# Another route for the decayed k of two attention units, and five smaller moves, in a gated linear attention and SwiGLU kernel on one core

## The chip, the cores and the metric

The kernel runs on one core of one Trainium2 chip. The metric is the device time of one execution in microseconds (us). The core has TensorE (PE in the profile, its weight loads PEld), VectorE (DVE), ScalarE (ACT), GpSimd (POOL) and SyncE (SP). SP, ACT and POOL also issue DMAs; each issues its own in program order.

## The reference, cut to what matters

All inputs to the attention are float32, the three weights float64. The attention is a recurrence with a decay for each channel; its output, with the heads side by side, is the input of a SwiGLU block.

```python
batch, n_heads, seq, head_dim = 4, 8, 768, 48
f = 1 / (1 + exp(-f_logit))
for t in range(S):
    state = f[:, :, t, :, None] * state + k[:, :, t] (x) v[:, :, t]
    y[:, :, t] = q[:, :, t] @ state
x = y.transpose(0, 2, 1, 3).reshape(3072, 384)
g = x @ w_gate                      # 384 x 1536
out = (g * sigmoid(g) * (x @ w_val)) @ w_out      # 1536 x 384
```

## The kernel before, in words

**Units.** The sequence is cut into six chunks c of 128 positions. A unit u = 4c + b is one chunk of one batch entry, all eight heads. The function `attention(u)` is a generator with some fifteen steps, so that the steps of a unit can be laid between the matrix products of the SwiGLU block for the chunk before. The steps are: sigmoid of f; f into the layout with channels on partitions; k likewise; a product scan from the back (`tail`, L630); kT, the k decayed to the end of its chunk (L576); the further route of kT for `turned` units (L646 to L650); a scan from the front (`gate`, L658); q into the layout; qT (L576 again); the scores kT against qT (L676); the causal mask on the scores (L691); the decayed state (L581); the output y (L712 and L716, or L737); the state's increment dS (L757), which needs kT with positions on partitions again, the tile `kt`; the new state (L766).

**Two routes to kt.** For a unit that isn't `turned`, four TensorE transposes (L680) put kT into a PSUM bank and ScalarE copies it to `kt` (L689). For a `turned` unit, VectorE transposes kT in blocks of 32 x 32 into the room that k was loaded to (`beside`, L646), four DMAs write it to DRAM (L649), and one DMA reads it back into `kt` in the right order (L687), issued in the step of the mask. In the kernel before, units 6 and 7 (GpSimd's queue) and 12 to 19 (SyncE's queue) are turned, units 0 to 5 and 8 to 11 are not, and the last chunk, 20 to 23, needs no `kt`. There is one `kt` buffer, so that its next writer waits for dS of the unit before. As `beside` lies in k's room, the k of the next unit is loaded (`load_after(u, "k")`) after the DMAs of L649 have read it, or right after the transpose of k (L622) where a unit isn't turned.

**The first stage (about 0 to 29 us)** runs the four units of chunk 0 with loads of f, k, q and v for each unit from SyncE's queue, and starts to fetch the weights. The weights come as float64; `weight_piece` turns each piece into float32 by ScalarE (L489, L491) and VectorE (the `join`: L500, L502, L504, then the sum L506 into w_both or w_out). Its order is written out by hand: `in_order` chains all instructions of TensorE, VectorE, ScalarE and SyncE as they are traced. GpSimd isn't in that chain; its instructions, such as the loads of v for units 6 and 7 (L455), are placed by the framework's own planned times.

**The second stage (about 29 to 140 us)** is the SwiGLU block of chunk 0 by plain products (`mlp_plain`: L812 for gate and val, L822 and L826 behind them, L835 for w_out), the rest of the weight pieces, sums of weights (L915, L918), and the units 4 to 7. Only a few of its instructions are chained by `keep_order` and `behind`; the rest is ordered by the framework's planned times.

**The third stage (from about 140 us)** does the SwiGLU block of chunks 1 to 5 by a fast matrix product: fifteen products of quarters and their sums for gate and val (`triple`, L1014, L1019, L915, L918, with L1030 and L966 behind them), in four rounds, then the product with w_out in seven parts (`down_seven`: one, six, two, three, four, five, seven, each in two halves; L1113 and L1176). Beside chunk c's block run the attention units of chunk c + 1. The order is by hand again, from a table of due times: each product counts 0.86, each half of a part of `down_seven` 1.95, and everything in `waiting` is traced when the sum of these has reached its time.

```python
    between = [n * TRIPLE - 0.05 for n in range(NJ)]                          # NJ = 4, TRIPLE = 12.9
    down = [NJ * TRIPLE + n * DOWN / 2 - 0.05 for n in range(14)]             # DOWN = 3.9
    return [[f, *steps, s + 0.02, s + masks[kind], s + 2.2, o, o + 0.01, o + 2.1] ...
    waiting += [(at, f) for at, f in zip(DOWN_SUMS_AT, down_weight_sums())]
```

`s` is a unit's time for the scores in `SCORES`, and also the time at which the output of the unit before is due (`o` of unit u is `s` of unit u + 1). `kind` says which PSUM banks the scores use: "A" are the two banks that the products and part three of `down_seven` also use. `SCORES` of the third chunk (c = 2) are 12, between[2], down[2] and down[6] for b = 0 to 3. `CHAINS` gives the times of the steps ahead of the scores. `down_weight_sums` makes four sums of halves of w_out (L918, tiles `ws` and w_out in place, 128 x 1152 each), which `down_seven` needs; they are due at `DOWN_SUMS_AT`. `in_order` chains TensorE, VectorE, ScalarE, GpSimd and SyncE in this stage as traced.

Of the kernel before, what the change touches and what calls it, by code (L numbers as in the profile page):

```python
# [9 lines left out]
FP32 = mybir.dt.float32  # L10
# [280 lines left out]
def short_path(ctx, tc, ident, least, judge, q, k, v, f_logit, moe_w_gate, moe_w_val, moe_w_out, out):  # L291
# [9 lines left out]
    nc = tc.nc  # L301
    B, H, S, D = q.shape
    C = 128
    NCH = S // C
    HP = H // 2
    W = 64
    DM = H * D
# [8 lines left out]
    SQUARES = 2  # L316
# [3 lines left out]
    att = ctx.enter_context(tc.tile_pool(name="att", bufs=1))  # L320
# [43 lines left out]
    def pairs(t, off=0):  # L364
        return t[:, off:off + HP * N1].rearrange("p (a t) -> p a t", t=N1)
# [35 lines left out]
    def by_squares(u):  # L401
        return u >= SQUARES * B - 2
# [6 lines left out]
    def v_of(u):  # L409
        return vs[u % (NV if units[u][1] < SQUARES else NV // 2)]  # L410
# [16 lines left out]

    traced = nc.cur_bb.bb.instructions
    by_pool = []

    def load(u, what="fkqv"):
        b, c = units[u]
        rows = slice(c * C, (c + 1) * C)
        inputs = dict(f=f_logit, k=k, q=q, v=v)
        for nm in "fqkv" if c >= SQUARES else "fvkq" if by_squares(u) else "fkqv":
            src = inputs[nm]
            if nm not in what:
                continue
            if nm == "v":
                dst = v_of(u)  # L440
            elif not by_squares(u):
                dst = raw[nm][u % NRAW]
            else:
                since = len(traced)
                for n in range(4):
                    at = Q * (1 - n % 2)
                    (nc.sync if c >= SQUARES else nc.gpsimd).dma_start(
                        out=rooms[nm][Q * n:Q * (n + 1), at:at + HP * RUN].rearrange("t (a e) -> t a e", a=HP),
                        in_=src[b, n // 2::2, rows, :].rearrange("a (t i) d -> t a (i d)", i=NI))
                if c < SQUARES:  # L450
                    by_pool.extend(ins for ins in traced[since:] if ins.engine == mybir.EngineType.Pool)
                    keep_order(by_pool[-5:])
                continue
            queue = nc.gpsimd if c < SQUARES and by_squares(u) else nc.sync
            queue.dma_start(out=dst[:, :, 0:D], in_=src[b, :, rows, :].rearrange("h t d -> t h d"))  # L455

    def weight_piece(dst, src, parts):

        b, a, n = dst.shape[1:]
        if src.dtype == FP32:
            by_row = src.rearrange("p a (b n) -> p a b n", n=n)
            return (lambda: [nc.sync.dma_start(out=dst[:, :, i], in_=by_row[:, i]) for i in range(a)]), [], []
        shape = [128, b // parts, a, n]
        kept = {}

        def fetch():  # L470
            kept["w"] = wst.tile([128, a, 2 * b * n], I32, tag="w64", name="w64", bufs=4)
            nc.sync.dma_start(out=kept["w"], in_=src)

        def part(m):
            return slice(m * b // parts, (m + 1) * b // parts)

        def halves(m):
            words = kept["w"].rearrange("p a (b n two) -> p a b n two", two=2, n=n)[:, :, part(m)].rearrange("p a b n two -> p b a n two")
            return words[:, :, :, :, 0], words[:, :, :, :, 1]

        def high_ends(m):
            quarters = kept["w"].bitcast(U16).rearrange("p a (b n four) -> p a b n four", four=4, n=n)[:, :, part(m)]
            return quarters.rearrange("p a b n four -> p b a n four")[:, :, :, :, 3]

        def sizes(m):
            lo, hi = halves(m)
            up = wst.tile(shape, I32, tag="up", name="up", bufs=NPART)
            ends = up.bitcast(U16).rearrange("p b a (n two) -> p b a n two", two=2)
            nc.scalar.activation(ends[:, :, :, :, 0], lo.bitcast(U32), AF.Copy, scale=2.0 ** -29)  # L489
            top = wst.tile(shape, I32, tag="top", name="top", bufs=NPART)  # L490
            nc.scalar.activation(top.bitcast(FP32), hi.bitcast(FP32), AF.Abs)  # L491
            kept["up", m], kept["top", m] = up, top

        def join(m, what=("clamp", "add")):
            lo, hi = halves(m)
            up, top = kept["up", m], kept["top", m]
            if "add" in what and "clamp" not in what:
                nc.vector.tensor_tensor(dst[:, part(m)].bitcast(I32), top, up, ALU.add)
                return
            nc.vector.tensor_scalar(top.bitcast(FP32), top.bitcast(FP32), as_float(0x38000000), as_float(0x47F00000),  # L500
                                    op0=ALU.max, op1=ALU.min)
            nc.vector.tensor_scalar(top, top, 3, 0x3FFFFFFF, op0=ALU.logical_shift_left, op1=ALU.bitwise_and)  # L502
            ends = up.bitcast(U16).rearrange("p b a (n two) -> p b a n two", two=2)
            nc.vector.tensor_single_scalar(ends[:, :, :, :, 1], high_ends(m), 0xC000, op=ALU.bitwise_and)  # L504
            if "add" in what:
                nc.vector.tensor_tensor(dst[:, part(m)].bitcast(I32), top, up, ALU.add)  # L506

        return fetch, [lambda m=m: sizes(m) for m in range(parts)], [lambda *what, m=m: join(m, *what) for m in range(parts)]

    def as_float(bits):  # L510
# [49 lines left out]
    def attention(u):  # L560
        b, c = units[u]
# [6 lines left out]
        in_squares = by_squares(u)  # L568

        def multiply(out, x, by):  # L570

            if in_squares:
                for_each = "p a (t j i) -> p a t j i"
                out, by = (t.rearrange(for_each, j=2, i=NI // 2) for t in (out, by))
                x = x.rearrange("p (j a t i) -> p a t j i", j=2, a=HP, i=NI // 2)
            nc.vector.tensor_tensor(out, x, by, ALU.mult)  # L576
# [35 lines left out]
            load_after(u, "f")  # L612
        yield

        turned = SQUARES < c < NCH - 1 or c < SQUARES and in_squares
        turn_queue = nc.sync if c >= SQUARES else nc.gpsimd
        kT = att.tile([128, HP, C], FP32, tag="kT", name="kT")
        qT = att.tile([128, HP, C], FP32, tag="qT", name="qT", bufs=2)
# [8 lines left out]
        n = HP * N1  # L627
# [14 lines left out]
        if turned:  # L642
# [4 lines left out]
            turn = turn_pool.tile([Q, NI, HP, NI, Q], FP32, tag="turn", name="turn")  # L647
            for r in range(NI):
                turn_queue.dma_start(out=turn[:, :, :, r, :].rearrange("t i a e -> t (i a) e"),  # L649
                                  in_=beside[Q * r:Q * (r + 1)].rearrange("t i (a e) -> t (i a) e", e=Q))  # L650
# [12 lines left out]
            load_after(u, "qv" if c < SQUARES else "q")  # L663
        yield
        multiply(qT, qp, pairs(gate)[:, :, 1:N1])
        nc.gpsimd.memset(pairs(gate)[:, :, 0:1], 0.0)  # L666
        if c < SQUARES:
            decay()
# [2 lines left out]
        A = att.tile([128, 2, HP, C], FP32, tag="A", name="A")  # L671
        sc = [score_bank(u) for _ in range(2)]
        for a in range(HP):
            for par in range(2):
                r = rows_of(par)
                nc.tensor.matmul(sc[par][:, a * C:(a + 1) * C], lhsT=kT[r, a, :], rhs=qT[r, a, :], start=True, stop=True)  # L676
        if c < NCH - 1 and not turned:
            p = bank("kt")
            for a in range(HP):
                nc.tensor.transpose(p[:, a * C:(a + 1) * C], kT[:, a, :], ident)  # L680
        yield
        if not in_squares:
            nc.scalar.copy(least[:, u, :], whole.rearrange("p a t -> p (a t)"))
        if c < NCH - 1:
            kt = att.tile([128, HP * C], FP32, tag="kt", name="kt")
            if turned:
                turn_queue.dma_start(out=kt, in_=turn.rearrange("t i a r e -> i t (a r e)"))  # L687
            else:
                nc.scalar.copy(kt, p)  # L689
# [10 lines left out]
        if c and b < B - 1:  # L700
# [8 lines left out]
            for a in range(HP):  # L709
                for par in range(2):  # L710
                    r = rows_of(par)
# [9 lines left out]
            for h in range(H):  # L721
                a, par = h // 2, h % 2
                f = h * D
                while f < (h + 1) * D:
                    n = min((h + 1) * D, (f // 128 + 1) * 128) - f
                    r = W * (a % 2) + f - h * D
                    (nc.gpsimd if c >= SQUARES else nc.sync).dma_start(out=xT[c][f % 128:f % 128 + n, f // 128, b * C:(b + 1) * C],  # L727
                                                                       in_=yT[r:r + n, par, a // 2 * C:(a // 2 + 1) * C])
# [60 lines left out]
    def keep_order(mine):  # L789
        for a, b in zip(mine, mine[1:]):  # L790
            tc.add_manual_dep(b, a.name, mybir.DependencyInfo(mybir.DependencyClass.NoSync,
                                                              mybir.DependencyReason.DATA), reason="order")
# [86 lines left out]
    def chain(k, q, qmul, turn=None, head=None):  # L879
# [3 lines left out]
    between = [n * TRIPLE - 0.05 for n in range(NJ)]  # L883
    down = [NJ * TRIPLE + n * DOWN / 2 - 0.05 for n in range(14)]
    SCORES = {c: scores for c, scores in zip(range(2, NCH), (
        ((12, "b"), (between[2], "o"), (down[2], "A"), (down[6], "A")),
        ((PRODUCT - 0.05, "b"), (between[1], "o"), (between[3], "o"), (down[3], "A")),
        *[((down[10] - whole, "A"), (between[1], "o"), (between[3], "o"), (down[3], "A"))] * (NCH - 4)))}
    CHAINS = {c: chains for c, chains in zip(range(2, NCH), (
# [18 lines left out]
        return {"o": banks_o, "A": banks_a}[kind].tile([128, 512], FP32, tag=kind, name="sc")  # L908

    FINISH = (3, 5, 6, 7, 9, 10)  # L910
    DOWN_SUMS_AT = (13.1, 26.5, 38, 48)
    sums = {}

    def plus(dst, a, b):
# [408 lines left out]

    waiting += [(at, f) for at, f in zip(DOWN_SUMS_AT, down_weight_sums())]
    blocks = {}
# [100 lines left out]
```

## Time and profile before

| what | us |
|---|---|
| median of three runs (600.44, 600.48, 600.49) | 600.48 |
| the profiled execution's own time | 600.68 |
| its span, first to last instruction | 599.0 |
| PE busy | 588.3 |
| DVE busy | 481.7 |
| ACT busy | 293.6 |
| POOL busy | 94.3 |

The span is what the profile's rows divide; the profiled execution took 1.7 us more than its span. Matmuls are pipelined and the profile models their ends, so that a row's busy time or mean duration is longer than the distance from one matmul to the next. For TensorE the start times of successive rows in the timeline are the measure. A timeline row is: start in us, duration in us, engine, line, operation, written tile <- read tiles, shape, count of merged instructions, and in brackets the idle time ahead of it with what ended it.

### The profile page before, as it was taken

Reading aid. Unit: us, or ns where it says so; the run is one execution under the profiler, and the core shown is the slowest. Engines: PE = TensorE matmul, PEld = TensorE weight load, DVE = VectorE, ACT = ScalarE, POOL = GpSimd, SP = SyncE. Lnnn points to the kernel's source line nnn. Section 1 sums busy time; section 2 is a strip of 40 time slices with the busy share of each in tenths; the row PEclk is TensorE's granted clock in tenths of the full one; section 3 lists DMA queues with packets and bytes.
Section 4 is the critical chain, followed back from the end, with each engine's and each line's share of the span. In section 5 each row is a group of like instructions: output and inputs, shape, how many; then the busy total and the mean of one; then the engine's idle time right before and its main releaser. Section 6 shows DMA issues by size and latency. Waiting matters only on the chain.

```text
span 599.0 us, 10862 instructions
## 1 busy us (share of the span) xinstructions
PE 588.3 (98%) x3996; PEld 485.4 (81%) x3996; DVE 481.7 (80%) x834; ACT 293.6 (49%) x558; POOL 94.3 (16%) x211
## 2 busy tenths in 40 slices
PE   7899999999999999999999999999999999999996
PEld 5744545667888899888899888899988899988896
DVE  7999998978999977998995978995878972666731
ACT  3577854115776422576740566632376730356600
POOL 1102225100030230121130030320030320000000
PEclk9999999999999999999999999999999999999999
DMA  9999664124331244442344432343230100100001
GB/s 198 252 274 319 199 182 116 25 77 132 81 83 49 51 110 112 133 97 70 98 116 108 126 76 68 98 112 99 82 102 26 28 10 6 54 1 1 1 1 55
DMA packets 104058, 57.33 MB, mean 96 GB/s; under 512 B 65632, under 2 KB 95712, under 8 KB 104000
## 3 DMA queue, kind: packets, MB, share of 16 engines
q1 hardware_dynamic: 95552, 46.09, 29.3%
q0 software_dynamic: 6432, 7.75, 4.4%
q10 hardware_dynamic: 2016, 2.75, 1.3%
q8 instruction: 32, 0.52, 0.4%
q14 instruction: 26, 0.21, 0.1%
HBM read 46.27 MB, written 7.34 MB: 90 GB/s over the span
## 4 chain that ended last, share of the span: by engine, by line
PE 86%; DVE 0%; issue 0%
PE o L1113 20%; PE A L1014 18%; PE B L1014 14%; PE c L1014 6%; PE o L1014 6%; PE o L835 5%; PE sc L676 3%; PE o L1176 3%; PE y L716 2%; PE gate L812 2%; PE val L812 2%; PE y L737 1%; PE y L712 1%; PE dS L757 1%; PE kt L680 0%; DVE A L691 0%
## 5 line engine op out<-in xcount | busy, mean ns | idle before, releaser
L727 POOL DMA_DIRECT2D xT<-yT x120 | 60.0, 507 | 51.0 <-ACT yT L720 45.2
L1014 PE MATMUL A<-xs,w_both 128*128 128x256 f32 x240 | 62.2, 382 | 0.0
L1113 PE MATMUL o<-w_out,h 128*128 128x192 f32 x360 | 62.0, 327 | 0.0
L1113 PEld LDWEIGHTS o<-w_out,h 128*128 128x128 f32 x360 | 58.7, 190 | 1.2 <-DVE h L966 0.3
L1019 ACT COPY c<-A 128x512 f32<-128x512 f32 x40 | 23.3, 583 | 60.7 <-PE A L1014 60.7
L1019 ACT COPY aside<-A 128x512 f32<-128x512 f32 x60 | 35.2, 586 | 34.1 <-PE A L1014 33.9
L915 DVE TENSOR_TENSOR c<-c,aside 128x512 f32<-128x512 f32 x60 | 41.1, 685 | 12.2 <-ACT aside L1019 10.7
L1014 PEld LDWEIGHTS A<-xs,w_both 128*128 128x128 f32 x240 | 44.9, 190 | 6.6
L966 DVE TENSOR_TENSOR h<-h,c 128x256 f32<-128x256 f32 x100 | 40.5, 414 | 7.6 <-ACT h L1030 7.3
L691 DVE TENSOR_TENSOR A<-sc,causal 128x512 f32<-128x512 f32 x48 | 31.0, 686 | 15.7 <-PE sc L676 15.7
L918 DVE TENSOR_TENSOR c<-c,aside 128x512 f32<-128x512 f32 x60 | 41.0, 683 | 2.2 <-ACT aside L1019 2.1
L1030 ACT ACTIVATE h<-c 128x256 f32<-128x256 f32 x100 | 39.2, 416 | 6.6 <-DVE c L915 5.1
L1113 PE MATMUL o<-ws,h 128*128 128x192 f32 x240 | 41.5, 328 | 0.2 <-DVE A L691 0.2
L666 POOL MEMSET gates<- 128x4 f32 x24 | 3.1, 128 | 243.7 <-DVE qT L576 237.5
L1014 PE MATMUL B<-xs,w_both 128*128 128x256 f32 x160 | 41.2, 380 | 0.0
L1014 PE MATMUL A<-xs,extra 128*128 128x256 f32 x160 | 41.2, 380 | 0.0
L1014 PE MATMUL c<-xT,w_both 128*128 128x256 f32 x160 | 41.1, 379 | 0.0
L1014 PE MATMUL B<-xT,extra 128*128 128x256 f32 x160 | 41.1, 379 | 0.0
L1113 PEld LDWEIGHTS o<-ws,h 128*128 128x128 f32 x240 | 39.1, 190 | 0.8 <-DVE A L691 0.4
L1019 ACT COPY aside<-B 128x512 f32<-128x512 f32 x60 | 35.1, 585 | 8.3 <-PE B L1014 7.1
L918 DVE TENSOR_TENSOR c<-o,c 128x512 f32<-128x512 f32 x40 | 27.4, 685 | 12.6 <-ACT h L1030 6.6
L915 DVE TENSOR_TENSOR c<-c,o 128x384 f32<-128x384 f32 x15 | 8.3, 552 | 36.3 <-PE o L1113 36.3
(154 smaller groups left out, 1224.3 us busy)
## 6 DMA issues: line engine op xcount, KB each, us to landing
fsquares<-in_f_logit_dram SPq DMA_DIRECT2D x64, 96.0 KB, 2.4
qsquares<-in_q_dram SPq DMA_DIRECT2D x64, 96.0 KB, 2.2
ksquares<-in_k_dram SPq DMA_DIRECT2D x64, 96.0 KB, 2.4
w<-in_moe_w_gate_dram SPq DMA_DIRECT2D x6, 768.0 KB, 6.2
w<-in_moe_w_val_dram SPq DMA_DIRECT2D x6, 768.0 KB, 5.3
w<-in_moe_w_out_dram SPq DMA_DIRECT2D x6, 768.0 KB, 6.9
v<-in_v_dram SPq DMA_DIRECT2D x22, 192.0 KB, 3.0
out_dram<-ob ACTq DMA_DIRECT2D x14, 192.0 KB, 2.0
```

What stands on the lines that cost most here:

```text
L676: nc.tensor.matmul(sc[par][:, a * C:(a + 1) * C], lhsT=kT[r, a, :], rhs=qT[r, a, :], start=True, stop=True)
L691: nc.vector.tensor_tensor(A[:, par], sc[par].rearrange("p (a t) -> p a t", t=C), causal.unsqueeze(1).broadcast_to((128, HP, C)), ALU.mult)
L727: (nc.gpsimd if c >= SQUARES else nc.sync).dma_start(out=xT[c][f % 128:f % 128 + n, f // 128, b * C:(b + 1) * C], in_=yT[r:r + n, par, a / ...
L812: nc.tensor.matmul(p, lhsT=w[:, j, i, :], rhs=xT[c][:, i, :], start=(i == 0), stop=(i == KT - 1))
L835: nc.tensor.matmul(p, lhsT=hidden_tile(h, n // 2)[:, n % 2 * 2 + b // 2, b % 2 * C:(b % 2 + 1) * C], rhs=w_out[:, j, :], start=(n == 0), s ...
L915: nc.vector.tensor_tensor(dst, a, b, ALU.add)
L918: nc.vector.tensor_tensor(dst, a, b, ALU.subtract)
L966: lagging.append(lambda: f(*args))
L1014: nc.tensor.matmul(p[name][:, n, :], lhsT=weights_of[a][:, n, j, :], rhs=tokens[b], start=fresh and n == 0, stop=True, skip_group_check=True)
L1019: nc.scalar.copy(t, p[name])
L1030: nc.scalar.activation(dst, src[:, 0, :], AF.Silu)
L1113: nc.tensor.matmul(p[:, n, :], lhsT=lhsTs[j][:, n * C:(n + 1) * C], rhs=rhs[:, j, :], start=first and j == order[0] and n == 0, stop=j == ...
```

## The change

It has six parts.

1. `turned` begins at unit 10 instead of unit 12: units 10 and 11, the last two of the third chunk, take the route by VectorE and DRAM.
2. For turned units from the third chunk on with b below 3, the DMA that reads `kt` back is issued in the step of the scores instead of the step of the mask. The tile `kt` is made in that step for every unit.
3. The scores of unit 11 are due at down[5] instead of down[6], that is one half part of `down_seven` earlier; with them goes the output of unit 10.
4. The four sums of w_out's halves are due at 1.4, 13.1, 26.5 and 48 instead of 13.1, 26.5, 38 and 48.
5. For pieces of w_out, VectorE's step L504 is placed behind qT of unit 5 (`first_scores`), as far as it is traced after it.
6. v of units 1 and 2 is loaded from GpSimd's queue instead of SyncE's.

```diff
+    first_scores = []
...
-            queue = nc.gpsimd if c < SQUARES and by_squares(u) else nc.sync
+            queue = nc.gpsimd if nm == "v" and c < SQUARES and (by_squares(u) or u in (1, 2)) else nc.sync
...
             nc.vector.tensor_single_scalar(ends[:, :, :, :, 1], high_ends(m), 0xC000, op=ALU.bitwise_and)
+            for ins in first_scores if n == DM else ():
+                keep_order([ins, traced[-1]])
...
-        turned = SQUARES < c < NCH - 1 or c < SQUARES and in_squares
+        turned = SQUARES * B + 2 <= u < (NCH - 1) * B or c < SQUARES and in_squares
...
         multiply(qT, qp, pairs(gate)[:, :, 1:N1])
+        if u == B + 1:
+            first_scores.append(traced[-1])
...
+        if c < NCH - 1:
+            kt = att.tile([128, HP * C], FP32, tag="kt", name="kt")
+        at_once = turned and c >= SQUARES and b < B - 1
+        if at_once:
+            turn_queue.dma_start(out=kt, in_=turn.rearrange("t i a r e -> i t (a r e)"))
         yield
         if not in_squares:
             nc.scalar.copy(least[:, u, :], whole.rearrange("p a t -> p (a t)"))
-        if c < NCH - 1:
-            kt = att.tile([128, HP * C], FP32, tag="kt", name="kt")
+        if c < NCH - 1 and not at_once:
             if turned:
                 turn_queue.dma_start(out=kt, in_=turn.rearrange("t i a r e -> i t (a r e)"))
...
-        ((12, "b"), (between[2], "o"), (down[2], "A"), (down[6], "A")),
+        ((12, "b"), (between[2], "o"), (down[2], "A"), (down[5], "A")),
...
-    DOWN_SUMS_AT = (13.1, 26.5, 38, 48)
+    DOWN_SUMS_AT = (1.4, 13.1, 26.5, 48)
```

## The prediction

> **What bounds the kernel now.** I read the page's busy times and chain first, then the chain of waits of PE, then the timelines around the places that the diff touches.
>
> ```profile
> PE 588.3 (98%) x3996; PEld 485.4 (81%) x3996; DVE 481.7 (80%) x834; ACT 293.6 (49%) x558; POOL 94.3 (16%) x211
> PE 86%; DVE 0%; issue 0%
> ```
>
> PE is the bound from its first gate product at 29.07 us to the end. Ahead of that, VectorE is: from 9.65 to 28 us its rows stand end to end. So a change pays only where it takes matmuls from PE's queue or ends one of PE's waits. The waits of PE, in the order of their sum:
>
> ```profile
> PE sc L676 <- DVE qT L576: 1.9, 2, 1.1
> ...
> PE sc L676 <- ACT top L491: 0.3, 1, 0.3
> PE y L737 <- issue: 0.3, 1, 0.3
> PE o L1113 <- DVE A L691: 0.2, 1, 0.2
> ```
>
> The 1.9 lies in the first stage. Behind it only two waits are named, the one put down to ACT's top and the one on A. Both lie where the change works.
>
> The first, in the timeline of all engines:
>
> ```profile
> 71.81 5.32 PE L812 MATMUL val<-xT,w_both 128*128 128x512 f32 x12
> ...
> 74.49 0.93 DVE L506 CUSTOM_DVE_ANT_0 w_out<-top,up 128x1536 uint16<-128x1536 uint16 x1
> ...
> 75.45 0.70 DVE L504 TENSOR_SCALAR up<-w 128x768 uint16<-128x768 uint16 x1
> ...
> 76.05 0.67 DVE L576 TENSOR_TENSOR kT<-kTp,tails 128x512 f32<-128x512 f32 x1
> ...
> 76.65 0.68 DVE L576 TENSOR_TENSOR qT<-qTp,gates 128x512 f32<-128x512 f32 x1
> ```
>
> This is unit 5. Its scores start on PE at 77.47, when qT is done (77.33). The last val product starts at 76.53 and takes the usual 0.43, so PE could have begun at 76.96: 0.51 lost. top L491 only ended nearby.
>
> The others, in PE's timeline:
>
> ```profile
> 170.28 1.16 PE L676 MATMUL sc<-qT,kT 48*128 48x128 f32 x16
> 171.37 0.66 PE L680 MATMUL kt<-idf,kT 128*128 128x128 f32 x4
> 171.86 1.03 PE L1014 MATMUL A<-xs,w_both 128*128 128x256 f32 x4
> 172.73 1.03 PE L1014 MATMUL B<-xs,w_both 128*128 128x256 f32 x4
> ...
> 204.38 1.16 PE L676 MATMUL sc<-qT,kT 48*128 48x128 f32 x16
> 205.47 0.66 PE L680 MATMUL kt<-idf,kT 128*128 128x128 f32 x4
> 205.97 4.07 PE L1113 MATMUL o<-ws,h 128*128 128x192 f32 x24
> ...
> 215.94 1.16 PE L676 MATMUL sc<-qT,kT 48*128 48x128 f32 x16
> 217.03 0.66 PE L680 MATMUL kt<-idf,kT 128*128 128x128 f32 x4
> 217.87 4.17 PE L1113 MATMUL o<-ws,h 128*128 128x192 f32 x24 [0.19 <-DVE A L691]
> ```
>
> Unit 10 goes from scores to products in 1.59, unit 11 in 1.93: 0.34 of waiting, because part three needs a bank of kind A and both hold unit 11's scores until VectorE has masked the first (217.13 to 217.82).
>
> **The change part by part.**
>
> *PE loses eight transposes (units 10, 11).* With them unit 9 needs 2.45 from scores to the second product (170.28 to 172.73). Unit 13, which is turned already, needs 2.06 (252.60 to 254.66). So a unit's four cost 0.39 net, and two units **0.78**. The Trainium skill (TensorE: Matmul & The Clock Gate, Part 4: PE-mode transpose) gives some 275 ns for one in a kernel, and the mean duration of L680 here is the same 273 ns; eight by that would be 2.2. But all four pass in 0.49, from 171.37 to the product's start at 171.86, so the rows decide: 0.78. The skill's rule (VectorE: DVE Perf Modes, Rules for kernel authors), to use TensorE for a 128 x 128 transpose where PSUM will do, speaks against the change; by it alone the sum would lack this term and carry VectorE's. Here VectorE has the gaps and PE hasn't, so I set it aside.
>
> *Unit 11's scores and unit 10's output come 1.95 earlier.* Then the second half of part two (twelve matmuls, 1.95) stands between the scores and part three, while the first mask needs 0.7. The wait goes: **0.34**.
>
> *VectorE for units 10 and 11:* two block transposes, 0.70 each in the row of L646 (0.6 from one start to the next). ScalarE loses two copies (0.59 each), which nobody waits for.
>
> *The sums of w_out's halves:* VectorE has no idle time from 174.7 to 199.9. The sum at 189.22 (1.26 to the next start) leaves that stretch, unit 10's transpose enters it: 0.66 less. This reaches the last h; PE's short wait for h at 200.47 (**0.17** over the usual step) should go. The sum that comes in at 1.4 falls on 142.2, where VectorE idles 0.89 ahead of 143.06. So 0.37 remains and lies on what follows until the next idle time at 174.7; unit 8's scores start at 152.40 with qT done at 151.53, so PE has 0.87 of room. Cost 0; without that room, up to 0.4.
>
> *qT of unit 11 is the tight place.* It was done at 213.14. In the new order PE, counted in the old clock, ends part one at 202.1, the scores of unit 10 at 205.3, part six at 209.3, half of two at 211.2, output and dS of unit 10 at 213.3, and then wants unit 11's scores. VectorE adds 0.6 for unit 11's transpose and saves the 0.66 above, so qT is done at about 213.1. I take 0; if the saving doesn't arrive, 0.6 of waiting, if more does, nothing is gained.
>
> *DRAM and SyncE.* Each unit adds four writes (2.6 of issue, 2.2 to landing) and one read (0.57). The read's landing:
>
> ```profile
> DMA to landing us min/median/max: 4.8/5.3/5.8
> ```
>
> The skill (DMA: Bandwidth & Descriptors, Anatomy of one DMA) would make 256 KB 2.6, so the row decides and the margin is smaller. Unit 10's read can issue when dS of unit 9 has freed the one kt buffer (204.4) and v of unit 11, also waiting for that, has gone (204.9); it lands by 210.8 at the latest, and dS of unit 10 wants it at 212.8.[...] Issued with the mask it would stand behind f of unit 12 and unit 11's writes, which wait for VectorE until 211: that order would cost PE 6. Unit 11's read, issued late as before, stands behind the loads of k, q and v of unit 12, at about 218, lands at 223.5; its dS comes at 229. What is moved later on SyncE is the next unit's k: for unit 11 to some 187 (needed 207), for unit 12 to 214 to 218 (needed at 219.9, with VectorE idle ahead of it). For units 12 to 18 the read passes at most the next f (1.8 of issue), which isn't needed for 10 us. Cost 0.
>
> *Unit 5.* Two L504 of w_out (0.60 at 70.15, 0.70 at 75.45) and the sum that hangs on the first (0.93 at 74.49) go behind qT: 2.2 less ahead of it, and 0.5 is needed. Gain **0.51**. Behind them wait ScalarE's L489 (75.50), which needs the freed buffer, and in its queue the silu at 77.23; that may slip by 1.9. PE needs the silu's bank at 81.6, so 3.8 of room.
>
> *v of units 1 and 2 on GpSimd.* GpSimd has nothing from 3.3 to 9.86, so both should go at once, a third of the way into the first loads. The DMA share is 1.01 to 1.12 in each 2 us from 2 to 12, at 200 to 225 GB/s, so 2 x 192 KB hold f, k and q of units 1 and 2 up by up to 1.8. f of unit 1 has 1.1 of room (its transposes at 6.77, the warm-up behind them ends at 8.76, the scores start at 9.88). So 0 to 0.7 of loss; SyncE wins 2.0 of issue, but no row of PE or VectorE before 29 us waits for what follows there. Below nothing: 0.2, if later loads come sooner. I take **+0.1**, near the row's end, since these loads land ahead of need.
>
> *Order of the second stage.* It is planned anew, which no row shows. From both sides: -0.2 (its small gaps) to +1.5 (half of the largest waits that VectorE has there, 3.6 and 2.9, turned onto PE). I take 0.
>
> Sum: -0.78 - 0.34 - 0.17 - 0.51 + 0.1 = -1.7. Against the profiled execution's 600.68 that is 599.0; the median is 0.2 lower, so 598.8.
>
> **The rivals.** This kernel's measurement can tell about 0.2%, 1.2 us, from no change.
>
> *Most of it is eaten* (0.25): the gain of 0.78 on PE is sure, but the start loses 0.7 and unit 11's qT 0.6, or a new wait of about 1 appears in the second stage. For: PE's slack is under 0.3 at unit 11. Against: the gain of the sum's move is in the same stretch. The sum -1.7 with 0.6 more at the start and 0.6 at unit 11 is -0.5, so 600.0; range 599.3 to 601.7.
>
> *ScalarE's queue in the second stage* (0.13), slower. If the planned order puts w_out's L504 and L506 not just behind qT of unit 5 but behind the VectorE work up to 84, L506 ends near 86 instead of 75.4. ScalarE's L489 then waits till 86 with the silu of 77.23 queued behind it, PE's gate product wants that bank at 81.6 and gets it at about 87.5. It decides from a delay of 3.8; at 10 it costs 6, less the 1.7: 604. For: VectorE is full there, and ScalarE already waits 1.25 and 1.78 ahead of two L489. Against: only 2.2 is to be moved.
>
> *The route by DRAM does not replace PE's work in time* is the same sign and smaller: it needs a landing over 7.6 where 5.8 is the largest seen. I leave 0.02 for it within the slower case.
>
> **How the numbers follow.** The forecast has 0.62, own range 598.1 to 599.2; the rivals 0.25 and 0.13. Low end 598.0 (start and second stage each 0.2 better, and a little). High end 601.0: it takes in the first rival but for its last part. The forecast is faster by over 0.2% (below 599.28), the first rival counts as the same, the second as slower.
>
> **What would show it.** In the changed profile: L680 x32 instead of x40; unit 5's scores within 0.1 of the last val product plus 0.43; no wait on A ahead of part three; units 10 and 11 with no idle PE at dS. I am wrong if a PE wait of over 0.5 stands at unit 11's scores or dS, if the first gate product starts later than 29.3, or if PE waits for a gate bank between 77 and 100.

## The result, and the profile after

The median went from 600.49 us (8 runs, 600.44 to 601.19) to 598.83 us (8 runs, 598.67 to 599.0): 1.66 us less, ratio 0.9971, 95% interval 0.9961 to 0.998. The profiled execution took 598.83 us, its span 597.0. Lines of the changed kernel stand 1 to 9 lower in the file than before (L491 is L492, L576 is L579, L676 L681, L680 L685, L691 L700, L1014 L1023, L1113 L1122).

The page of the changed kernel, first its row of busy times, then that of its chain:

```profile
PE 586.5 (98%) x3988; PEld 483.8 (81%) x3988; DVE 482.7 (81%) x836; ACT 292.3 (49%) x556; POOL 95.2 (16%) x213
...
PE 98%; DVE 1%; ACT 0%; issue 0%; DVEq 0%
```

PE is busy 1.8 less and is still the bound; VectorE has two block transposes more, ScalarE two copies less. The waits of PE (us in total, times, longest):

```profile
PE sc L681 <- DVE qT L579: 2.3, 2, 1.5
...
PE sc L681 <- ACT least L693: 0.5, 1, 0.5
PE y L746 <- issue: 0.4, 1, 0.4
PE sc L681 <- ACT state L773: 0.4, 1, 0.4
```

The two waits that the prediction named, on ACT's top and on A, are gone, and no new kind stands in their place: all these rows lie in the first stage, and from 30 us to the end the list is empty. The row on qT is longer because the warm-up matmuls ahead of it ended earlier; unit 0's scores start at 9.88 as before.

Where the time came from is read by laying the start of each matmul beside that of the same matmul before. The difference, from the start of the span on:

| place | step, us | sum, us |
|---|---|---|
| y of unit 3 (27.3) | +0.12 | +0.12 |
| scores of unit 5 (77) | -0.42 | -0.29 |
| after the last h of the third chunk (200) | -0.28 | -0.58 |
| behind the scores of unit 10 (205) | -0.39 | -0.97 |
| around the scores of unit 11 (213 to 218) | -0.70 | -1.67 |
| last matmul | 0 | -1.68 |

From 27 us on, no other place adds more than a few hundredths. PE's timeline of the stretch that the change is about:

```profile
203.80 1.16 PE L681 MATMUL sc<-qT,kT 48*128 48x128 f32 x16
204.90 4.17 PE L1122 MATMUL o<-ws,h 128*128 128x192 f32 x24
208.90 2.11 PE L1122 MATMUL o<-w_out,h 128*128 128x192 f32 x12
210.94 0.67 PE L721 MATMUL y<-qT,decayed 48*64 48x128 f32 x16
211.54 1.09 PE L725 MATMUL y<-A,v 128*64 128x128 f32 x16
212.47 0.62 PE L766 MATMUL dS<-v,kt 128*64 128x48 f32 x16
213.16 1.16 PE L681 MATMUL sc<-qT,kT 48*128 48x128 f32 x16
214.25 2.22 PE L1122 MATMUL o<-w_out,h 128*128 128x192 f32 x12
216.31 4.06 PE L1122 MATMUL o<-ws,h 128*128 128x192 f32 x24
```

After the scores of unit 10 the product with w_out starts 1.10 later, against 1.59 (204.38 to 205.97) with the transposes between. Of these 0.49, 0.39 is gained: straight behind scores, the product's first matmul takes 0.26 to the next one (204.90 to 205.16), behind the transposes it took the usual 0.16. Unit 11's scores come before the second half of part two, and part three at 216.31 follows without a wait. No wait stands at dS of unit 10 or 11, so `kt` is back in time. VectorE beside it:

```profile
212.32 0.69 DVE L579 TENSOR_TENSOR qT<-tails,gates 128x512 f32<-128x512 f32 x1
214.33 1.29 DVE L700 TENSOR_TENSOR A<-sc,causal 128x512 f32<-128x512 f32 x2 [1.31 <-PE sc L681]
```

qT of unit 11 is done at 213.01. dS started at 212.47 and elsewhere takes 0.55 to the next start (203.25 to 203.80), so PE could have begun the scores at 213.02 and began at 213.16. The place is as tight as that: 0.14 was lost there.

### The profile page after: what moved, and what is told of

Read it like the earlier page. It is cut to its first block, busy times and chain, and to the rows that moved or that the text cites. A ratio compares the mean times of both kernels' runs of the same rounds, so it can differ in the third digit from the quotient of the medians.

```text
span 597.0 us, 10869 instructions
## 1 busy us (share of the span) xinstructions
PE 586.5 (98%) x3988; PEld 483.8 (81%) x3988; DVE 482.7 (81%) x836; ACT 292.3 (49%) x556; POOL 95.2 (16%) x213
## 4 chain that ended last, share of the span: by engine, by line
PE 98%; DVE 1%; ACT 0%; issue 0%; DVEq 0%
PE o L1122 20%; PE A L1023 18%; PE B L1023 14%; PE o L1023 6%; PE c L1023 6%; PE o L844 5%; PE gate L821 5%; PE val L821 5%; PE sc L681 4%; PE o L1185 3%; PE y L725 3%; PE y L746 2%; PE dS L766 2%; PE y L721 2%; PE kt L685 1%; PE fTp L599 0%
## 5 line engine op out<-in xcount | busy, mean ns | idle before, releaser
L1023 PE MATMUL A<-xs,w_both 128*128 128x256 f32 x240 | 62.2, 382 | 0.0
L1122 PE MATMUL o<-w_out,h 128*128 128x192 f32 x360 | 62.0, 327 | 0.0
L1122 PEld LDWEIGHTS o<-w_out,h 128*128 128x128 f32 x360 | 58.7, 190 | 1.0 <-issue 0.2
L1023 PEld LDWEIGHTS A<-xs,w_both 128*128 128x128 f32 x240 | 44.9, 190 | 6.6
L700 DVE TENSOR_TENSOR A<-sc,causal 128x512 f32<-128x512 f32 x48 | 31.0, 685 | 14.4 <-PE sc L681 14.4
L1122 PE MATMUL o<-ws,h 128*128 128x192 f32 x240 | 41.5, 328 | 0.0
L1023 PE MATMUL A<-xs,extra 128*128 128x256 f32 x160 | 41.2, 380 | 0.0
L1023 PE MATMUL B<-xs,w_both 128*128 128x256 f32 x160 | 41.2, 380 | 0.0
L1023 PE MATMUL c<-xT,w_both 128*128 128x256 f32 x160 | 41.1, 379 | 0.0
L1023 PE MATMUL B<-xT,extra 128*128 128x256 f32 x160 | 41.1, 379 | 0.0
L1122 PEld LDWEIGHTS o<-ws,h 128*128 128x128 f32 x240 | 39.1, 190 | 0.5
```

Source lines behind the costliest of these rows:

```text
L700: nc.vector.tensor_tensor(A[:, par], sc[par].rearrange("p (a t) -> p a t", t=C), causal.unsqueeze(1).broadcast_to((128, HP, C)), ALU.mult)
L1023: nc.tensor.matmul(p[name][:, n, :], lhsT=weights_of[a][:, n, j, :], rhs=tokens[b], start=fresh and n == 0, stop=True, skip_group_check=True)
L1122: nc.tensor.matmul(p[:, n, :], lhsT=lhsTs[j][:, n * C:(n + 1) * C], rhs=rhs[:, j, :], start=first and j == order[0] and n == 0, stop=j == ...
```

## The experiments

Ten other kernels ran, and the changed one again. Each kernel's median is of 5 to 12 executions; matmul times are those of one profiled execution each. "TensorE" is the start of the last matmul against the changed kernel's 592.00; the kernel before has +1.68. "Time" is the difference of medians to the kernel before, run beside it.

| kernel | TensorE, us | time, us | ratio, 95% interval |
|---|---|---|---|
| changed | 0 | -1.66 | 0.9971 [0.9961, 0.998] |
| changed, again | 0.00 | -1.77 | 0.9969 [0.9957, 0.9981] |
| part 1 undone (not_turned) | +0.63 | -1.05 | 0.9986 [0.9977, 0.9995] |
| part 2 undone (at_mask) | +0.64 | -1.19 | 0.9974 [0.9963, 0.9985] |
| part 3 undone (late_scores) | +0.72 | -0.87 | 0.9984 [0.9975, 0.9993] |
| part 4 undone (old_sums) | +1.22 | -0.45 | 0.9993 [0.9984, 1.0002] |
| part 5 undone (no_first) | +0.39 | -1.34 | 0.9978 [0.9969, 0.9987] |
| part 6 undone (v_back) | -0.13 | -1.45 | 0.9977 [0.9967, 0.9986] |
| parts 1 and 2 alone (turn_only) | +2.00 | +0.60 | 1.0008 [1.0, 1.0017] |
| units 8 and 9 turned too (turn8) | +0.73 | -0.65 | 0.9985 [0.9976, 0.9993] |
| unit 9 turned in a gap (late9) | -0.42 | -2.02 | 0.9963 [0.995, 0.9977] |
| and part 6 undone (late9_v) | -0.53 | -2.12 | 0.9961 [0.9947, 0.9975] |

The end of the program varies. From the last matmul's start to the end of the span the profiles show 5.0 us in the changed kernel, 5.2 when it ran again, 5.3 in the kernel before, 5.5 in v_back and in turn_only, and 5.9 in turn8, though no edit touches what comes there. VectorE's last row ends 0.72 after that start in each of them, so the difference lies behind it, where the last output is written and the program ends; its cause stays open. Differences of a few tenths are therefore read from the matmuls: in the two profiles of the changed kernel these start within 0.02 of each other from 9.88 us on. By the intervals of the ratios only old_sums and turn_only stand apart from the changed kernel.

### Part 6 undone: v of units 1 and 2 by SyncE

```diff
-            queue = nc.gpsimd if nm == "v" and c < SQUARES and (by_squares(u) or u in (1, 2)) else nc.sync
+            queue = nc.gpsimd if nm == "v" and c < SQUARES and by_squares(u) else nc.sync
```

> The changed kernel with v of units 1 and 2 on SyncE's queue again (part 6 undone); every other engine keeps its order. Theory, terms add up place by place: only the first stage can differ. If its 0.12 of loss belongs to the moved loads, the first gate product starts at 29.07 again and the time is 598.7. If the 0.12 is a chance meeting of GpSimd's load of v for unit 6 (24.78) with VectorE's L501, it may stay or go, 598.7 to 598.85. Rival, SyncE's freed queue brings the weights earlier and the second stage lives on it: without it a wait appears between 29 and 140, 599.1 or more.

TensorE's first gate product starts at 29.07 as before, against 29.20, and the 0.13 stays to the end. The median was nevertheless no better (599.13); in the profile that is the program's end, 0.53 longer. The rival's number was met without its cause: between 29 and 140 us no wait appears. The 0.13 arises at 25 us. VectorE's timeline of the changed kernel:

```profile
25.12 0.70 DVE L501 TENSOR_SCALAR top<-top 128x384 f32<-128x384 f32 x1
25.86 0.36 DVE L503 TENSOR_SCALAR top<-top 128x384 int32<-128x384 int32 x1
26.13 0.59 DVE L505 TENSOR_SCALAR up<-w 128x384 uint16<-128x384 uint16 x1
26.61 1.27 DVE L700 TENSOR_TENSOR A<-sc,causal 128x512 f32<-128x512 f32 x2
```

The same stretch with part 6 undone:

```profile
25.11 0.35 DVE L501 TENSOR_SCALAR top<-top 128x384 f32<-128x384 f32 x1
25.50 0.60 DVE L503 TENSOR_SCALAR top<-top 128x384 int32<-128x384 int32 x1
26.02 0.57 DVE L505 TENSOR_SCALAR up<-w 128x384 uint16<-128x384 uint16 x1
26.49 1.26 DVE L700 TENSOR_TENSOR A<-sc,causal 128x512 f32<-128x512 f32 x2
```

In both, one of the first two rows, which usually take 0.35, takes 0.60 or 0.70, while GpSimd issues v of unit 6 (from 24.78, for 0.88 in the changed kernel and 1.16 in the other). In the changed kernel it is the first row and the longer loss; the mask behind it, and so y of unit 3, comes 0.12 later. In the profiles of four kernels with v of units 1 and 2 on SyncE the first gate product starts at 29.07 to 29.09, of nine with it on GpSimd at 29.14 to 29.46. In all four the second row is hit (0.60), in all nine the first (0.67 to 0.71). That the part costs this is shown. Why it decides which VectorE row is hit is only argued: with v of units 1 and 2 on SyncE this load is GpSimd's first, and its issue takes 1.16; in the changed kernel the first is at 3.23 (1.04) and this one takes 0.88, so its phases lie otherwise against VectorE's rows. The Trainium skill (SBUF — State Buffer, Who interferes with whom) has GpSimd and a two-port VectorE operation shut each other out for a whole instruction. That fits only in part: with part 6 undone, L501 runs at its usual 0.35 (25.11 to 25.46) inside GpSimd's issue (24.78 to 25.94), so it isn't the whole of the issue that holds VectorE up. No run here shows the lock itself.

### Part 5 undone: unit 5's qT behind w_out's L505 again

```diff
-            for ins in first_scores if n == DM else ():
+            for ins in ():
```

> The changed kernel without the ordering of w_out's step behind qT of unit 5 (part 5 undone). Theory, terms add up: unit 5's scores wait for qT again, 0.42 more, 599.25, and nothing else moves. Rival, the second stage was planned anew to the good elsewhere as well, or to the bad: more than 599.5, or less than 599.0.

The scores of unit 5 start at 77.56 instead of 77.17, and the difference of 0.39 stays to the end. The wait of before is back in the list of waits:

```profile
PE sc L681 <- ACT top L492: 0.3, 1, 0.3
```

### Part 4 undone: the sums of w_out's halves at their old times

```diff
-    DOWN_SUMS_AT = (1.4, 13.1, 26.5, 48)
+    DOWN_SUMS_AT = (13.1, 26.5, 38, 48)
```

> The changed kernel with the sums of w_out's halves at their old times (part 4 undone). Theory, the sums pay for the transposes on VectorE: the wait for h near 200 returns and grows (0.28 and up to 0.6 more for unit 10's transpose), and qT of unit 11 comes 0.6 to 1.2 later, on top of its wait of 0.13: 1.0 to 1.8 more in all, 599.8 to 600.6. Rival, each part on its own: only the 0.28 at h returns, 599.1.

PE falls behind by 0.13 at 192, by 0.94 from 200 on and by 1.20 at the scores of unit 11. PE's timeline with part 4 undone shows where most of it is:

```profile
197.87 2.76 PE L1122 MATMUL o<-w_out,h 128*128 128x192 f32 x16
201.18 1.57 PE L1122 MATMUL o<-w_out,h 128*128 128x192 f32 x8 [0.55 <-DVE h L975]
```

The last h of the chunk is late, and then qT of unit 11. With unit 10's block transpose in the stretch without VectorE idle time and no sum taken out of it, nearly all of the change's gain is gone.

### Part 3 undone: unit 11's scores where they were

```diff
-        ((12, "b"), (between[2], "o"), (down[2], "A"), (down[5], "A")),
+        ((12, "b"), (between[2], "o"), (down[2], "A"), (down[6], "A")),
```

> The changed kernel with unit 11's scores due at down[6] again (part 3 undone). Theory: part three waits for a bank of kind A until the first mask is done, and the four transposes that used to fill part of that time are gone, so 0.7 to 0.8 of waiting stands there; the wait for qT of unit 11 (0.13) goes. Net 0.6 to 0.7 more, 599.4 to 599.5. Rival, the gain at unit 11 is the removed transposes and not the bank: 0.2 more or less, 598.7 to 599.0.

PE's timeline:

```profile
214.98 1.16 PE L681 MATMUL sc<-qT,kT 48*128 48x128 f32 x16
216.92 4.17 PE L1122 MATMUL o<-ws,h 128*128 128x192 f32 x24 [0.78 <-DVE A L700]
```

From scores to product it is 1.94, as in the kernel before with its transposes (1.93). Part three starts when VectorE has masked the first bank; whether four transposes lie in that time or not makes no difference. Without part 3, turning unit 11 gains nothing.

### Part 2 undone: the reading back issued with the mask

```diff
-        at_once = turned and c >= SQUARES and b < B - 1
+        at_once = False
```

> One thing undone against the changed kernel: the reading back of unit 10's decayed k is issued where its scores are masked (due 57) and no longer at once behind the write's stage, so on SyncE it stands behind the load of unit 12's f. Theory now: it stands behind that one load alone (issued about 205.6, 1.8 us), is issued at about 207.4 in place of 204.5, takes 4.8 to 5.8 us as the other readings back do, and lands at 212.2 to 213.2 against the product into the state at 212.47: TensorE waits 0 to 0.8 us, 598.8 to 599.6. Rival (the prediction's own claim): it stands behind unit 11's writes too (its turned k at 210.6, 2.6 us), lands at about 218, and TensorE waits some 6 us there: 604 to 605.

SyncE's queue, and then the row at which PE waits, in the timelines of this kernel:

```profile
205.83 1.74 SPq L448 DMA_DIRECT2D fsquares<-in_f_logit_dram  x4
207.68 0.67 SPq L696 DMA_DIRECT2D kt<-turn  x1
210.87 2.98 SPq L652 DMA_DIRECT2D turn<-ksquares  x4
```

```profile
213.19 0.67 PE L766 MATMUL dS<-v,kt 128*64 128x48 f32 x16 [0.29 <-DMA kt<-turn]
```

The reading stands behind f of unit 12 alone and not behind unit 11's writes. It is issued at 207.68, and PE's dS starts 5.5 later. Of the 0.64 on TensorE, 0.27 arises in the first stage (first gate product at 29.46), where this edit changes nothing; 0.37 is left for part 2 after the scores of unit 11, which no longer wait for qT. The wait of 6 that the prediction named isn't there.

### Part 1 undone: both units transposed by TensorE, all else kept

```diff
-        turned = SQUARES * B + 2 <= u < (NCH - 1) * B or c < SQUARES and in_squares
+        turned = SQUARES * B + 4 <= u < (NCH - 1) * B or c < SQUARES and in_squares
```

> One thing undone against the changed kernel: both units are again transposed by TensorE; the sums' new times, the earlier scores of unit 11, unit 5's order and v by GpSimd stay. Theory (each transposed unit costs TensorE what its step shows, 0.39 us, and the kernel with it hides the VectorE work): +0.39 at unit 10, and at unit 11 +0.39 less the 0.13 us that its scores wait for qT in the changed kernel: +0.65, that is 599.4 to 599.6, faster than before by some 1.0 us. Rival (the gain is the freed VectorE's and the scores' order; the transposes ran in time that TensorE has to wait out anyway): within 0.2 us of the changed kernel.

+0.39 behind the scores of unit 10, -0.15 at the scores of unit 11 (no wait for qT), +0.39 behind them: +0.63.

### Parts 1 and 2 alone on the kernel before

Parts 3 to 6 are undone together, each by the diff above.

> Parts one and two alone on the kernel before: k of units 10 and 11 turned by VectorE and DRAM; the sums, unit 11's scores, unit 5's order and v's queue as before. Theory (the turning pays only with the other edits): -0.39 at unit 10; at unit 11 what the transposes took is waited for at the bank of A instead, about 0; and VectorE's two more transposes with no sum taken off it make the matmuls wait some 0.6 us longer for h: 600.4 to 600.9, no gain. Rival (each part's gain stands alone): -0.78 us, 599.7.

The median, 601.29, is 0.60 above the kernel before and over the 600.4 to 600.9 expected. TensorE's last matmul is 0.32 later; most of the rest is the end of the program. Waits of PE in this kernel (its L1120 is the product with w_out):

```profile
PE o L1120 <- DVE A L698: 0.8, 1, 0.8
PE o L1120 <- DVE h L973: 0.5, 1, 0.5
```

The first was 0.2 before: what unit 11's transposes took is waited for instead. The second is new: unit 10's block transpose delays h. Unit 10 gains its 0.39, h takes 0.54 and small steps the rest.

### Units 8 and 9 turned too

```diff
-        turned = SQUARES * B + 2 <= u < (NCH - 1) * B or c < SQUARES and in_squares
+        turned = SQUARES * B <= u < (NCH - 1) * B or c < SQUARES and in_squares
```

> The changed kernel, with units 8 and 9 of the third chunk turned in the same way: eight more transposes off TensorE, two more 32x32 block transposes and no copy by ScalarE. Theory (TensorE's step is the gain wherever VectorE keeps the scores' inputs in time): -0.39 at each unit, 598.0 to 598.2. Rival (VectorE has no idle time between 143 and 173 us of the changed kernel, so each block transpose of about 0.7 to 1.1 us put there delays what stands behind it, the q of unit 9 and the gated h): a new wait of 0.5 to 1.5 us takes the gain, 598.6 to 599.6.

PE is 0.57 ahead at 160 and 1.14 behind from 165 on, then gains 0.4 at unit 9: +0.73 at the end. The chain, from this kernel's timelines of VectorE, ScalarE and PE in turn:

```profile
162.40 0.71 DVE L649 STREAM_TRANSPOSE ksquares<-kT 128x512 f32<-128x512 f32 x1
163.03 1.19 DVE L661 TENSOR_TENSOR_SCAN gates<-gates,start 128x516 f32<-128x516 f32 x1
164.15 0.40 DVE L975 TENSOR_TENSOR h<-h,c 128x256 f32<-128x256 f32 x1
```

```profile
164.63 0.58 ACT L1028 COPY c<-c 128x512 f32<-128x512 f32 x1 [2.22 <-DVE h L975]
```

```profile
165.27 1.13 PE L1023 MATMUL c<-xT,w_both 128*128 128x256 f32 x4 [1.45 <-ACT c L1028]
```

VectorE's h at 164.15 is at 162.81 in the changed kernel: two block transposes (unit 8's at 147.32 was the other) of 0.6 to 0.7 from start to start, with next to no gap between 143 and 173 to take them in. ScalarE's copy of product c is released by that h, and the product c behind needs the bank. The two units' gain of some 1.0 costs 1.7.

### Unit 9 turned where VectorE is idle

The block transpose goes behind the mask and the decayed state of unit 9, into the `kt` tile itself (k's room is wanted by the next load by then), and SyncE writes it and reads it back at once. Unit 8 stays with TensorE.

```diff
+        late_turn = u == SQUARES * B + 1
...
-        if c < NCH - 1 and not turned:
+        if c < NCH - 1 and not turned and not late_turn:
...
-        if c < NCH - 1 and not at_once:
+        if c < NCH - 1 and not at_once and not late_turn:
...
         if c >= SQUARES:
             decay()
+        if late_turn:
+            turn = turn_pool.tile([Q, NI, HP, NI, Q], FP32, tag="turn", name="turn")
+            nc.vector.transpose(kt.rearrange("p (i a e) -> p a i e", e=Q, a=HP), kT.rearrange("p a (i e) -> p a i e", e=Q))
+            for r in range(NI):
+                nc.sync.dma_start(out=turn[:, :, :, r, :]..., in_=kt[Q * r:Q * (r + 1), :]...)
+            nc.sync.dma_start(out=kt, in_=turn.rearrange("t i a r e -> i t (a r e)"))
         yield
```

> The changed kernel with unit 9 turned too, but its block transpose put behind its mask, where VectorE sits idle 1.31 us (173.1 to 174.4), and not behind its k at 162, where it cost 1.4 us of waiting when units 8 and 9 were turned. Written and read back by SyncE at once; its product into the state is about 30 us later. Theory (the turning pays by TensorE's own step, 0.39 us, where VectorE has idle time for the block transpose): 598.4 us, TensorE 0.39 us earlier from 171 on. Rival (every block transpose in the second stage is paid for in waits): no gain or a loss of up to 0.7 us, 598.8 to 599.5.

VectorE's timeline:

```profile
173.03 0.70 DVE L708 STREAM_TRANSPOSE kt<-kT 128x512 f32<-128x512 f32 x1
174.03 0.69 DVE L935 TENSOR_TENSOR c<-o,c 128x512 f32<-128x512 f32 x1 [0.30 <-PE o L1031]
```

The transpose lies in what was idle, with 0.30 left over. PE is 0.39 ahead from 171 on and 0.42 at the last matmul. The same edit with v of units 1 and 2 back on SyncE:

> As the one before, with v of units 1 and 2 back on SyncE (the sixth part undone). Theory (v by GpSimd only brings the collision of its issue with VectorE at 25 us, 0.13 us, and nothing at the end): TensorE 0.13 us earlier from 27 on, 598.3 us. Rival (v by GpSimd is worth the 0.3 us that the median without it was longer): 598.7 us.

TensorE is ahead by another 0.11 from 27 us on. And the changed kernel as it is, in the same job:

> The changed kernel as it is, beside the two below. Theory: as before, 598.8 us, 0.997 of the kernel before; what the median does beside the last matmul's start shows how far the end of the program (the last output's landing) varies by itself: 0.3 us either way.

Medians: 598.96 for the changed kernel, 598.71 with unit 9 turned in the gap, 598.61 with part 6 undone as well; the ranges (598.78 to 599.07, 598.54 to 598.91, 598.35 to 598.65) of the first and the last don't touch. The last one beats both kernels of this study: the changed one by 0.35 in the median and by 0.53 on TensorE.

## Why the prediction was right or wrong, point by point

The predicted 598.8 and the sum of -1.7 were met (598.83; -1.66 by the medians, -1.68 by TensorE), and the signs named for it came out: 32 transposes by TensorE instead of 40, unit 5's scores within 0.1 of the place named, no wait on A, none at dS, the first gate product ahead of 29.3. That the sum was met to a few hundredths is in part luck: two waits were worth 0.11 more each than said, unit 5 gave 0.09 less, and qT of unit 11 cost 0.14 where 0 was taken. These errors cancel. The steps:

- **PE loses eight transposes, 0.78.** Right: 0.39 behind unit 10's scores, twice in not_turned, and in late9 for another unit; the price of the Trainium skill (TensorE: Matmul & The Clock Gate, Part 4: PE-mode transpose), 275 ns each (beside a figure for bf16; here it is float32), would have made it 1.1 for a unit, so the rows were the better guide. But it isn't a gain that stands alone, as the sum takes it and the rival "most of it is eaten" says ("the gain of 0.78 on PE is sure"): in late_scores unit 11's 0.39 brings nothing, and in turn_only both together end 0.32 behind. The costs of undoing parts 1, 2, 3, 4 and 5 (0.63, 0.37, 0.72, 1.22, 0.39) less the 0.13 of part 6 add up to 3.2, about twice the gain: the parts hold each other up.
- **Unit 11's scores, 0.34.** Right: the wait on A is gone. Of the 0.70 gained around these scores, 0.39 for the transposes and the 0.14 lost at qT leave 0.45 for it, more than was said: after the wait, part three's first matmul took 0.27 to the next (217.87 to 218.14) instead of 0.16, and that went with it.
- **The sums' move, 0.17.** Right in kind, 0.28 in size. The same 24 matmuls around the last h, before and after:

```profile
198.04 4.34 PE L1113 MATMUL o<-w_out,h 128*128 128x192 f32 x24
...
197.74 4.06 PE L1122 MATMUL o<-w_out,h 128*128 128x192 f32 x24
```

They lost the wait (200.47 to 200.81) and also the slow start behind it (0.27 to the next matmul), which the step over the usual distance doesn't hold.

- **Where the moved sum lands.** Wrong, without effect on the number. It was put "on 142.2, where VectorE idles 0.89"; it ran earlier, and that idle time is still there. VectorE's timeline of the changed kernel:

```profile
138.31 1.36 DVE L927 TENSOR_TENSOR ws<-w_out 128x1152 f32<-128x1152 f32 x1
139.57 1.11 DVE L865 COPY ob<-o 128x384 f32<-128x384 f32 x2
140.60 0.68 DVE L924 TENSOR_TENSOR w_both<-w_both 128x512 f32<-128x512 f32 x1
141.20 0.68 DVE L927 TENSOR_TENSOR w_both<-w_both 128x512 f32<-128x512 f32 x1
142.77 0.69 DVE L927 TENSOR_TENSOR c<-o,c 128x512 f32<-128x512 f32 x1 [0.89 <-ACT c L1028]
```

Before, VectorE waited 1.10 in that stretch for PE:

```profile
139.13 0.56 DVE L856 COPY ob<-o 128x384 f32<-128x384 f32 x1 [0.37 <-PE o L835]
140.42 0.56 DVE L856 COPY ob<-o 128x384 f32<-128x384 f32 x1 [0.73 <-PE o L835]
```

The sum took this idle time: the first copy came 0.44 later, but the rows from 140.60 on came earlier than before, and none of PE's rows waited. So the 0.37 that the prediction wanted covered by unit 8's room never came up.

- **qT of unit 11, cost 0 (0 to 0.6).** It cost 0.14, a term put at nothing; qT was done at 213.01 where about 213.1 was said, and PE wanted the scores at 213.02.
- **DRAM and SyncE, 0.** Right. The read of unit 11 was issued at 218.09 (about 218 was said), and PE waits at no dS. But the landings of 4.8 to 5.8 from which this was read aren't those of SyncE's reads. The trace has a landing for two reads into kt only, those of units 6 and 7, which GpSimd issues at 97.73 and 119.55. In the changed kernel's view of the tile kt it is these two again:

```profile
DMA to landing us min/median/max: 5.1/5.3/5.5
```

For a read by SyncE only at_mask has a figure: 5.5 from its issue to the dS that waits for it. So the margin was about right, but read from rows of another queue. The 2.6 that the prediction sets beside it is an estimate from a fit that the Trainium skill (DMA: Bandwidth & Descriptors, Anatomy of one DMA) gives for DMAs by GpSimd; it speaks of those two reads, and for them it is too low.

The aside "Issued with the mask it would stand behind f of unit 12 and unit 11's writes", at a cost to PE of 6, was wrong: in the table of due times the mask (down[2] + 1.5) comes after f of unit 12 but ahead of unit 11's transposes. At_mask measured a cost of 0.37.

- **Unit 5, 0.51.** 0.42 in the change, 0.39 by no_first. The direction and place were right; the term was sized with the step of one val product to the next, 0.43, and the scores still start 0.09 after that (76.65 + 0.43 = 77.08, against 77.17). In the changed kernel qT is done at 75.59, so VectorE no longer sets it; what does is open. Its timelines of PE, VectorE and ScalarE in turn:

```profile
71.93 5.32 PE L821 MATMUL val<-xT,w_both 128*128 128x512 f32 x12
77.17 1.16 PE L681 MATMUL sc<-qT,kT 48*128 48x128 f32 x16
...
74.92 0.67 DVE L579 TENSOR_TENSOR qT<-qTp,gates 128x512 f32<-128x512 f32 x1
75.52 0.59 DVE L505 TENSOR_SCALAR up<-w 128x768 uint16<-128x768 uint16 x1
...
73.22 1.09 ACT L831 ACTIVATE h<-gate 128x512 f32<-128x512 f32 x2
77.19 1.09 ACT L490 ACTIVATE up<-w 128x768 uint16<-128x768 uint32 x1 [2.88 <-issue]
```

The silu that was to slip from 77.23 came earlier instead: it is the second of the two at 73.22, as the new order has it ahead of L490. L490 alone slipped, from 75.50 to 77.19, and no gate product waited.

- **v on GpSimd, +0.1.** The size was right, the reason wrong. Contention at the first loads was named; the first scores start at 9.88 in both profiles. The loss arises at 25 us, on VectorE. The loads' contention may be there too: in several runs with v on GpSimd PE waits some 1.0 at f's transposes (1.0 to 1.4 at 6.4), and the first scores still start on time. In at_mask f's second transposes (17.57 to 18.30) are late too, and 0.27 gets through. But late9_v, with v on SyncE, shows waits of up to 0.5 at f's transposes as well, so the runs don't tell this apart.
- **Order of the second stage, 0.** Right: between unit 5's scores and 200 us no matmul moved against its neighbours by more than 0.03. The slower rival, ScalarE's queue, didn't occur: L505 of w_out was moved behind qT and no further (75.52), and the silu stood ahead of L490.

## What to carry to other kernels

Moving a layout change off the engine that bounds pays by that engine's own step from start to start (0.39 here, not four times the 0.27 us duration), and only if the other engine has idle time for it before someone waits: the same block transpose gained 0.39 in a 1.31 us gap and, with that of another unit, lost 0.73 where there was none. Before taking work out of a bounding engine's queue, ask whether a wait lies behind it, for then the wait grows by what was taken out; first move what ends the wait. When several edits share a stretch, undo them one at a time: here each of four was worth 0.4 to 1.2, and the two about the transposes alone gained nothing (TensorE ended 0.32 later).

## What was not expected of the hardware

- In every profile one VectorE row of 128 x 384 took 0.60 to 0.71 us instead of 0.35 while GpSimd issued one load (0.88 to 1.19 us). Which of two rows it was made the 0.13 us that part 6 costs.
- The time from the last matmul's start to the end of the span varied between 5.0 and 5.9 us with nothing changed there.
- Behind a wait, or straight behind scores, a product's first matmul took 0.26 to 0.27 us to the next instead of 0.16. Ending the waits of 0.17 and 0.34 was worth 0.28 and some 0.45.
